# The conditioning vector's load moved to the ScalarE DMA queue, ahead of a transformer block on one core

## The chip, the cores and the metric

The kernel runs on one core of a Trainium2 chip. The metric is the device time of one execution, in microseconds (us). Each execution also has a span: the time from the first to the last recorded activity on the core, some 2.4 us shorter than the device time here. The span can be compared with times inside the trace.

## The reference

The block is a conditioned transformer block in bf16, with 2048 tokens and a width of 1024. A vector `c` is turned into six rows of modulation (shift, scale and gate for each of the two halves):

```python
mod = (silu(c) @ w_mod).reshape(1, 6, 1, -1)
sa, ca, ga, sb, cb, gb = mod[:, 0], ..., mod[:, 5]
h = layernorm(x) * (1 + ca) + sa
x = x + ga * linear_attention(h, wqkv, wo)      # 32 heads, phi(t) = elu(t) + 1
h = layernorm(x) * (1 + cb) + sb
x = x + gb * ((silu(h @ w_gate) * (h @ w_up)) @ w_down)   # width 3584
```

Only the opening matters here: the first row tiles of `x` (128 tokens each) are normalised, transposed, scaled with `ca`, shifted with `sa`, and multiplied by the Q part of `wqkv`.

## The kernel before

The kernel records its operations in a list, works out the semaphores, and emits one program per engine in the order of recording. All loads come from one queue, SyncE's, in this order:

```python
P.dma("c", CS8[0:NDT, :], cv8)                       # the vector, 2 KB
for st in range(4):
    P.dma("x0_%d" % st, XRES[:, st, :], xv[:, st, :])  # four x tiles, 256 KB each
ca_load(0)          # 1 MB of w_mod, columns of ca ("wca")
wq_load(0, 2)       # 512 KB of wqkv
ca_load(1)
wq_load(2, 2)
sa_load(1)          # 1 MB of w_mod, the upper half of sa ("wsa")
wq_load(4)          # 256 KB each
...                 # wq_load 5, 6, 7
sa_load(0)
# ... further x tiles and the K part of wqkv
```

The vector is transposed by TensorE, goes through Silu on ScalarE and is copied by VectorE. Then come the statistics of the x tiles, and between them TensorE runs "fillers": matmuls on zeros, whose result nobody reads, to keep it active.

```python
P.pe("transpose", out=PSB[:, 1, 0:NDT], in_=CS8[0:NDT, :], identity=IDENT[0:NDT, 0:NDT])
P.act("activation", out=SILUC[:], in_=PSB[:, 1, 0:NDT], func=ACT.Silu)
P.dve("tensor_copy", out=SILUF[:], in_=SILUC[:])
# ...
act_stats(2)                 # tile 2: sums on ScalarE
# ...
warm(13, bank=3)             # 13 fillers
# ... statistics of tiles 0 and 1 on VectorE, tile 0 normalised
tile_transposes(0)
warm(5, bank=3)              # 5 fillers
# ... tile 1 normalised on ScalarE
tile_transposes(1)
warm(1, bank=3)              # 1 filler
# ... tiles 2 and 3 normalised
mod_sc(WCA, 8, range(2))     # first modulation matmuls: silu(c) with ca's columns
fin_ca(0, 2)
tile_transposes(2, 3)
```

After this the Q matmuls follow, with more modulation matmuls between them. The first shift matmuls (`mod_sc` on `WSA`, columns 512 to 767) stand behind 26 of the Q matmuls and need the load `sa_load(1)`.

## Time and profile before

| | kernel before |
|---|---|
| device time, median of 3 | 836.26 us (834.89 to 836.29) |
| span of the profiled execution | 833.0 us |
| TensorE busy | 821.9 us, 99% |
| chain that ended last | 94% TensorE |
| TensorE idle before its first instruction | 2.2 us |

These are the head of the profile page, its busy times by engine, and its last chain, for the kernel before. "PEclk" on the page is at full rate in all slices. (The trace's first clock event, the grant of the full rate, is at 6.59 us; the page takes the time before it as full too.)

```profile
span 833.0 us, 10031 instructions
PE 821.9 (99%) x4053; PEld 379.9 (46%) x4132; DVE 301.7 (36%) x659; ACT 196.2 (24%) x335; POOL 43.6 (5%) x56
PE 94%; DVE 3%; DMA 1%; SPq 1%; issue 1%; ACT 0%; DVEq 0%; ACTq 0%
```

TensorE (PE) bounds the kernel. A change of the opening can only win what TensorE loses there. The timeline of the opening shows it. Its columns are: start in us, duration in us, engine, source line, operation, what it writes `<-` what it reads, shape and count; in brackets the idle time just before it on its engine, and what ended that. "SPq" is SyncE issuing a DMA.

```profile
0.79 0.40 SPq L178 DMA_DIRECT2D cs<-in_c_dram  x1
1.24 1.78 SPq L178 DMA_DIRECT2D xres<-in_A_x_dram  x4
2.42 0.18 ACT L178 ACTIVATE siluc<-ps 128x8 bf16<-128x8 bf16 x1 [0.35 <-PE ps L178]
4.03 1.94 DVE L178 BATCH_NORM_STATS2 stats<-xres 128x6 f32<-128x512 bf16 x3 [1.23 <-DMA xres<-in_A_x_dram]
6.28 1.06 ACT L178 ACTIVATE ht<-xres 128x1024 bf16<-128x1024 bf16 x1 [3.68 <-DMA xres<-in_A_x_dram]
8.79 0.56 SPq L178 DMA_DIRECT2D wsa<-in_w_mod_dram  x1
...
10.50 0.38 PE L178 MATMUL ps<-e,ident 128*128 128x512 bf16 x1
10.93 0.55 PE L178 MATMUL ps<-siluc,wca 128*128 128x1 bf16 x16
20.08 0.55 PE L178 MATMUL ps<-siluc,wsa 128*128 128x1 bf16 x16 [0.44 <-DMA wsa<-in_w_mod_dram]
28.42 1.89 PE L178 MATMUL ps<-ht,wqk 128*128 128x512 bf16 x8
```

Read from the top: the vector's issue holds SyncE for 0.40 us, and the x tiles' issues start at 1.24 us. VectorE waits for x until 4.03 us, and ScalarE waits for tile 2 until 6.28 us. TensorE waits 0.44 us for the shift weights at 20.08 us. From the last line on, TensorE runs without a wait of note to the end, which comes 833.0 - 28.42 = 804.6 us later. I call that line the end of the opening.

The windows view says what the loads do meanwhile. Its columns are: the window, its length, busy time of PE, PEld, DVE, ACT and POOL, the granted TensorE clock, the busy share of the DMA engines, and GB/s.

```profile
4.00:6.00 2.00, 2.00 (x6) 0.76 (x5) 1.97 (x4) 0.00 (x0) 0.00 (x0) 1.00 0.95 285
10.00:12.00 2.00, 1.89 (x34) 1.42 (x35) 1.24 (x4) 0.00 (x0) 0.78 (x1) 1.00 1.07 376
```

The DMA engines are full (share 0.95 and 1.07), and the loads land in the order of their issue: the first load of `wca` is complete at 10.88 us, the upper half of `wsa` at 20.04 us.

### The profile page before, as it was taken

Reading aid. Unit: us, or ns where it says so; the run is one execution under the profiler, and the core shown is the slowest. Engines: PE = TensorE matmul, PEld = TensorE weight load, DVE = VectorE, ACT = ScalarE, POOL = GpSimd, SP = SyncE. Lnnn points to the kernel's source line nnn. Section 1 sums busy time; section 2 is a strip of 40 time slices with the busy share of each in tenths; the row PEclk is TensorE's granted clock in tenths of the full one; section 3 lists DMA queues with packets and bytes.
Section 4 is the critical chain, followed back from the end, with each engine's and each line's share of the span. In section 5 each row is a group of like instructions: output and inputs, shape, how many; then the busy total and the mean of one; then the engine's idle time right before and its main releaser. Section 6 shows DMA issues by size and latency. Waiting matters only on the chain.

```text
span 833.0 us, 10031 instructions
## 1 busy us (share of the span) xinstructions
PE 821.9 (99%) x4053; PEld 379.9 (46%) x4132; DVE 301.7 (36%) x659; ACT 196.2 (24%) x335; POOL 43.6 (5%) x56
## 2 busy tenths in 40 slices
PE   7999999999999999999999999999999999999998
PEld 4544444454444444444444444444444444444444
DVE  5797985657873211110222211122111212111111
ACT  3667642223332111110211111111111111111011
POOL 1000000000050000030000003000000300000000
PEclk9999999999999999999999999999999999999999
DMA  9969734928197995610455571045557004553000
GB/s 312 298 149 228 205 74 146 200 103 303 34 222 241 255 272 152 177 51 13 114 152 152 151 186 42 13 113 153 152 152 198 28 13 119 152 154 93 1 26 25
DMA packets 190940, 117.17 MB, mean 141 GB/s; under 512 B 49576, under 2 KB 174640, under 8 KB 190896
## 3 DMA queue, kind: packets, MB, share of 16 engines
q1 hardware_dynamic: 190896, 116.55, 50.7%
q8 instruction: 32, 0.52, 0.3%
q14 instruction: 12, 0.10, 0.0%
HBM read 100.67 MB, written 4.33 MB: 126 GB/s over the span
## 4 chain that ended last, share of the span: by engine, by line
PE 94%; DVE 3%; DMA 1%; SPq 1%; issue 1%; ACT 0%; DVEq 0%; ACTq 0%
PE ps L178 94%; DMA wsa<-in_w_mod_dram 1%; DVE acc L178 1%; SPq L178 1%; DVE xres L178 0%; DVE pkt L178 0%; DVE mhl L178 0%; DVE ht L178 0%; DVE e L178 0%; DVE pqt L178 0%; ACT e L178 0%; ACT mw L178 0%; DVE ve L178 0%; DVE modcol L178 0%; DVE ut L178 0%
## 5 line engine op out<-in xcount | busy, mean ns | idle before, releaser
L178 PE MATMUL ps<-h2t,guu 128*128 128x512 bf16 x878 | 210.1, 379 | 0.9
L178 PE MATMUL ps<-h2t,gug 128*128 128x512 bf16 x878 | 209.9, 379 | 0.9
L178 DVE TENSOR_TENSOR at<-sg,ps 128x512 bf16<-128x512 bf16 x112 | 77.0, 687 | 296.2 <-PE ps L178 285.1
L178 ACT ACTIVATE sg<-ps 128x512 bf16<-128x512 f32 x112 | 66.9, 597 | 310.3 <-PE ps L178 298.9
L178 PEld LDWEIGHTS ps<-h2t,guu 128*128 128x128 bf16 x896 | 87.7, 98 | 105.7
L178 PEld LDWEIGHTS ps<-h2t,gug 128*128 128x128 bf16 x896 | 87.5, 98 | 105.3
L178 PE MATMUL ps<-wd_a,at 128*128 128x512 bf16 (+2 forms) x519 | 112.8, 372 | 0.5
L178 PE MATMUL ps<-ht,wqk 128*128 128x512 bf16 x498 | 110.7, 379 | 1.0 <-DVE ht L178 0.3
L178 PE MATMUL ps<-wd_b,at 128*128 128x512 bf16 (+2 forms) x388 | 85.4, 372 | 0.5
L178 PEld LDWEIGHTS ps<-wd_a,at 128*128 128x128 bf16 x528 | 51.1, 98 | 59.8
L178 PEld LDWEIGHTS ps<-ht,wqk 128*128 128x128 bf16 x512 | 49.3, 98 | 58.7 <-DVE mv L178 0.3
L178 DVE TENSOR_TENSOR ut<-att,gb_b 128x512 bf16<-128x512 bf16 (+1 forms) x32 | 13.8, 432 | 167.3 <-ACT att L178 167.3
L178 ACT ACTIVATE att<-ps 128x512 bf16<-128x512 f32 (+1 forms) x32 | 17.4, 591 | 182.1 <-PE ps L178 182.1
L178 PEld LDWEIGHTS ps<-wd_b,at 128*128 128x128 bf16 x396 | 38.3, 98 | 44.6
L178 PE MATMUL ps<-pk,xres 128*128 128x512 bf16 x250 | 56.2, 379 | 0.4 <-issue 0.2
L178 PE MATMUL ps<-mw,pqt 128*128 128x512 bf16 x250 | 55.8, 379 | 0.4
L178 POOL TENSOR_SCALAR h2t<-h2t,modcol 128x512 bf16<-128x512 bf16 x32 | 28.6, 912 | 394.9 <-DMA h2t<-xn 378.6
L178 ACT ACTIVATE e<-ps 128x512 bf16<-128x512 f32 x56 | 33.0, 602 | 32.8 <-PE ps L178 27.3
L178 PEld LDWEIGHTS ps<-mw,pqt 128*128 128x128 bf16 x256 | 24.9, 98 | 29.7 <-DVE xres L178 0.2
L178 PEld LDWEIGHTS ps<-pk,xres 128*128 128x128 bf16 x256 | 24.8, 98 | 29.8 <-issue 0.4
L178 ACT ACTIVATE junk<-xres 128x1024 bf16<-128x1024 bf16 x24 | 25.4, 1059 | 36.0 <-DVE xres L178 35.8
L178 POOL TENSOR_TENSOR rstd<-ve,neghalf 128x1 f32<-128x1 f32 (+2 forms) x17 | 14.2, 850 | 215.7 <-DVE ve L178 176.4
(101 smaller groups left out, 342.5 us busy)
## 6 DMA issues: line engine op xcount, KB each, us to landing
gug<-in_B_w_gate_dram SPq DMA_DIRECT2D x56, 512.0 KB, 4.0
guu<-in_B_w_up_dram SPq DMA_DIRECT2D x56, 512.0 KB, 5.3
xres<-in_A_x_dram SPq DMA_DIRECT2D x20, 256.0 KB, 8.0
rb<-recip_den SPq DMA_DIRECT2D x8, 512.0 KB, 11.9
stgx<-in_w_mod_dram SPq DMA_DIRECT2D x2, 2048.0 KB, 8.8
wd_a<-in_B_w_down_dram SPq DMA_DIRECT2D x4, 1024.0 KB, 7.5
out_dram<-xres SPq DMA_DIRECT2D x31, 128.0 KB, 1.7
xres<-in_A_x_dram SPq DMA_DIRECT2D x3, 1024.0 KB, 14.5
```

Source lines behind the costliest of these rows:

```text
L178: return getattr(e, method)(**kw)
```

## The change

Its intent: the vector's issue leaves SyncE's queue, so that the first x tile heads it; and a filler goes that would then stand in the way. The short description speaks of "the first filler matmuls", but the diff drops one filler, the third group; the 13 and the 5 stay. The rest of the diff is bookkeeping: since ScalarE now also issues a DMA, a recorded operation carries a flag for "is a DMA" where the engine's name used to tell.

```diff
-        P.dma("c", CS8[0:NDT, :], cv8)
+        P.dma("c", CS8[0:NDT, :], cv8, queue="act")
@@
-        warm(1, bank=3)
+        warm(0, bank=3)
@@ bookkeeping, one of several places
-            if op.eng not in self.COMPUTE and op.fn is not None:
+            if op.isdma and op.fn is not None:
```

In the built program the vector's load is ScalarE's first instruction, ahead of its table load and of Silu.

More of the change, by code (lines that the diff above doesn't have):

```diff
@@ L96 @@
 class _Op:
-    __slots__ = ("idx", "eng", "fn", "deps", "signaled", "count", "semkey", "waits", "ninc", "tag")
+    __slots__ = ("idx", "eng", "fn", "deps", "signaled", "count", "semkey", "waits", "ninc", "tag", "isdma")
     def __init__(self, idx, eng, fn, semkey, ninc, tag):
@@ L109, in __init__ @@
         self.tag = tag
+        self.isdma = semkey.startswith("lane:")
 def _is_ap(v):
@@ L129, in add @@
     def add(self, eng, fn, reads=(), writes=(), lane=None, ninc=1, tag=None):
-        if eng in self.COMPUTE:
-            semkey = eng
-        else:
-            assert lane is not None
-            semkey = "lane:" + lane
+        semkey = eng if lane is None else "lane:" + lane
+        assert eng in self.COMPUTE or lane is not None
         op = _Op(len(self.ops), eng, fn, semkey, ninc, tag)
@@ L165, in add @@
         self.by_eng.setdefault(eng, []).append(op)
-        if eng not in self.COMPUTE:
+        if op.isdma:
             self.dma_ops.append(op)
@@ L216, in resolve @@
             if op.signaled:
-                c = counters.get(op.semkey, 0) + (op.ninc if op.eng in self.COMPUTE else 16 * op.ninc)
+                c = counters.get(op.semkey, 0) + (16 * op.ninc if op.isdma else op.ninc)
                 counters[op.semkey] = c
@@ L236, in resolve @@
                 sn = dict(kn)
-                if op.eng in self.COMPUTE:
+                if not op.isdma:
                     sn[op.semkey] = op.count
@@ L253, in body @@
                     if op.signaled:
-                        if eng in self.COMPUTE:
+                        if not op.isdma:
                             r.then_inc(sems[op.semkey], op.ninc)
```

## The prediction

> **What bounds it.** The page gives a span of 833.0 us with TensorE busy 821.9 us (99%) at the full granted clock; the chain that ended last is 94% TensorE. From about 20 us to the end TensorE hardly waits: the waits view lists only some 4.5 us of TensorE idle time worth naming, 2.2 us of it before the first instruction, none over 0.2 us after 21 us. In the opening 20 us the loads bound it: the windows view shows the DMA share at 0.94 to 1.09 from 3 us on (240 to 380 GB/s), and the chain of waits over the first 45 us runs through SyncE's issues and the load of the shift weights (wsa) to 20.04 us.
>
> **What the change does.**
> 1. The conditioning vector's issue (0.79 us, 0.40 us long on SyncE) leaves the SyncE queue. The x tiles, issued from 1.24 us, and all loads after them then move up by 0.45 us. [...] I count only that; the trace of before has one issuing engine, so it cannot confirm it.
> 2. ScalarE gets the issue, ahead of its first table load (1.28 us, now at 0.79). Silu (now at 2.42) comes 0.2 to 0.4 us later. VectorE needs the Silu result for its copy (2.63 us) ahead of the first statistics; those wait for x until 4.03 us, about 3.6 us after the change. About 0.5 us of slack is left, so no cost.
> 3. Though the title says fillers, the diff drops only one, between the transposes of tile 1 and the first modulation matmuls (10.50 us, 0.38 us). The weight load behind it was released by wca at 10.93 us, so dropping it alone gains nothing; it only clears the way once wca lands near 10.5 us.
>
> **How it adds up.** x lands about 0.45 us earlier, so statistics, tile 2's sums on ScalarE (started by x at 6.28 us) and the transposes of tile 1 (10.05 us, released by ScalarE) move up alike. wca lands about 0.45 earlier, wsa too (TensorE waits for it at 20.08 us). The transposes of tile 0 gain only 0.2 us (the 13 fillers still end at 7.61 us), hidden behind the wait for ScalarE. Clock warm-up: fillers stand about 0.43 us apart until 6.6 us, then 0.27 or less. [...] it is untouched. From 20 us on everything keeps its length and is shifted.
>
> Gain about 0.45 us of 836 (0.05%), below the scatter of the three runs (834.89 to 836.29). The runs average about 835.8; I predict 835.4 us, range 834.2 to 836.6; faster by over 2% 0.005, within 2% 0.99, slower 0.005.
>
> **What would show each step.** The timeline: first x issue near 0.8 us; first statistics near 3.6 us instead of 4.03; first modulation matmul near 10.5 instead of 10.93; first shift matmul near 19.6 instead of 20.08. TensorE's busy time falls by about 0.4 us.
>
> **What would make it wrong.** The vector landing late on the ScalarE queue (behind x packets), which would hold the fillers and the VectorE copy and thus the statistics; the first x transfer not starting earlier because something other than the issue sets the first arrival; another packet interleaving that delays wca or wsa. Each is tenths of a us.

The sum is the 1.24 - 0.79 = 0.45 us by which the x issue moves up. The fillers' spacing changes at 6.6 us, and the trace of before has the grant of the full clock at 6.59 us.

## The result

The changed kernel took 834.90 us in the median (834.55 to 835.88, 4 runs), the kernel before 835.62 us in the median of its 4 runs of that comparison. The ratio is 0.9993 with a 95% interval of 0.9976 to 1.0011. Ratios here are the mean time of one kernel's fast runs over that of the other's of the same rounds, so they are not quite the ratio of the medians.

The profiled execution was the slowest of the four. Its page:

```profile
span 833.4 us, 10108 instructions
PE 825.8 (99%) x4131; PEld 379.8 (46%) x4131; DVE 301.9 (36%) x659; ACT 196.0 (24%) x335; POOL 43.3 (5%) x56
PE 96%; DMA 1%; DVE 1%; SPq 1%; issue 0%; ACT 0%; DVEq 0%
```

TensorE's busy time did not fall by 0.4 us, it rose by 3.9 us. That shows no cost: the count of recorded matmuls rose from 4053 to 4131 although one matmul was dropped. The trace of before lacks 79 records (4132 weight loads, 4053 matmuls). Busy sums of these two traces can't be compared to a few tenths.

The timeline of the opening, changed kernel, same execution ("ACTq" is ScalarE issuing a DMA):

```profile
0.79 1.82 SPq L176 DMA_DIRECT2D xres<-in_A_x_dram  x4
0.79 0.58 ACTq L176 DMA_DIRECT2D cs<-in_c_dram  x1
2.70 0.18 ACT L176 ACTIVATE siluc<-ps 128x8 bf16<-128x8 bf16 x1
3.66 1.88 DVE L176 BATCH_NORM_STATS2 stats<-xres 128x6 f32<-128x512 bf16 x3 [0.58 <-DMA xres<-in_A_x_dram]
6.31 1.06 ACT L176 ACTIVATE ht<-xres 128x1024 bf16<-128x1024 bf16 x1 [3.44 <-DMA xres<-in_A_x_dram]
7.95 0.59 SPq L176 DMA_DIRECT2D wsa<-in_w_mod_dram  x1
...
10.28 0.54 PE L176 MATMUL ps<-siluc,wca 128*128 128x1 bf16 x16
20.43 0.55 PE L176 MATMUL ps<-siluc,wsa 128*128 128x1 bf16 x16 [0.76 <-DMA wsa<-in_w_mod_dram]
28.77 1.45 PE L176 MATMUL ps<-ht,wqk 128*128 128x512 bf16 x6
```

The first steps are as predicted: x is issued at 0.79 us, the statistics start 0.37 us earlier, the first modulation matmul 0.65 us earlier. But tile 2 reaches ScalarE no earlier (6.31 against 6.28 us), and wsa, issued 0.84 us earlier, releases TensorE 0.35 us later. So this execution's opening ends 0.35 us later than in the trace of before. From there to the end it takes 833.4 - 28.77 = 804.6 us, as before. The windows view of the changed kernel shows the DMA engines full as well:

```profile
4.00:6.00 2.00, 2.00 (x6) 0.76 (x5) 1.97 (x6) 0.00 (x0) 0.01 (x1) 1.00 0.99 332
10.00:12.00 2.00, 1.29 (x32) 1.15 (x30) 1.18 (x4) 0.00 (x0) 0.78 (x1) 1.00 1.10 352
```

The questions were: is the head start real, what is it worth, and why is it not in this trace?

### The profile page after: what moved, and what is told of

Read it like the earlier page. It is cut to its first block, busy times and chain, and to the rows that moved or that the text cites. A ratio compares the mean times of both kernels' runs of the same rounds, so it can differ in the third digit from the quotient of the medians.

```text
span 833.4 us, 10108 instructions
## 1 busy us (share of the span) xinstructions
PE 825.8 (99%) x4131; PEld 379.8 (46%) x4131; DVE 301.9 (36%) x659; ACT 196.0 (24%) x335; POOL 43.3 (5%) x56
## 4 chain that ended last, share of the span: by engine, by line
PE 96%; DMA 1%; DVE 1%; SPq 1%; issue 0%; ACT 0%; DVEq 0%
PE ps L176 96%; DMA wsa<-in_w_mod_dram 1%; SPq L176 1%; DVE acc L176 0%; DVE xres L176 0%; DVE mhl L176 0%; ACT mw L176 0%; DVE ve L176 0%; DVE ut L176 0%; DVE mean L176 0%; DVE msq L176 0%; DVE sumx L176 0%; DVEq L247 0%
```

## The experiments

Theory "shift": everything moves by the time that the head of the queue was held. Rival "absorption": the opening waits for loads whose landing scatters more than the head start, so that the gain is lost. All kernels gave the right result. The record has the span of every execution of the experiments, and in all traces the rest after the opening takes 804.6 to 804.7 us, so the span tells to about 0.1 us when the opening ended.

### The same two kernels again

Edit: none. `after_again` and `after_third` are the changed kernel, `before_again` is the kernel before.

> The changed kernel again, unedited. Shift theory (all loads and all work move up by the 0.45 us that the vector's issue took): mean time 0.3 to 0.6 us below the kernel before, and in the trace the first shift matmul (wsa) starts between 19.4 and 19.8 us. Absorption theory (the opening waits for loads whose landing scatters by more than the head start; in the first trace of after wsa landed at 20.4 us although it was issued 0.84 us earlier): the mean is within 0.2 us of before, and the wsa matmul starts anywhere from 19.5 to 20.5 us.

> The kernel before again, unedited, as a measure of noise: ratio 1.000 within 0.0007 (0.6 us). Its trace shows how much the landing of x tile 2 (6.28 us in the first trace) and of wsa (20.04 us) scatter with nothing changed: absorption theory 0.3 us or more, shift theory below 0.15 us.

> The changed kernel a third time, for the size of the gain: the span lies 0.3 to 0.6 us below that of the kernel before in the mean (shift theory, 0.45), and every execution's span follows from where the opening ended, so that the time from the bias matmuls to the end is 804.5 to 804.8 us as in all traces so far.

| run | median us | before, same chip | ratio, 95% | spans |
|---|---|---|---|---|
| after_again | 834.81 | 835.34 | 0.9999 (0.9987 to 1.0012) | 831.8 to 835.0 |
| before_again | 834.96 | 835.34 | 0.9997 (0.9985 to 1.0008) | 832.4 to 833.2 |
| after_third | 835.35 | 835.27 | 1.0006 (0.9993 to 1.0018) | 832.4 to 834.8 |

One comparison can't resolve the effect. Taken together, over the executions whose spans the record lists (those of the experiments, and the first four of the changed kernel): two of 45 executions of the kernel before and two of 15 of the changed one have a mean granted clock of 0.998 instead of 1.000 and spans of 834.8 to 835.3 us. They are treated below (see the dose experiment); both kernels have them. Without them the mean span is 832.87 us for the kernel before (43 executions, standard error 0.06) and 832.57 us for the changed one (13, standard error 0.14): a gain of 0.30 us, with a 95% interval of about 0.0 to 0.6. With them the difference of the means is 0.09 us, and is not resolved. The figure also pools chips. On chip 4 the changed kernel's five full-clock executions are 0.58 us below the 16 of the kernel before; on chip 12 its four are 0.11 us above the nine. So the size of the gain rests on few executions.

In the traces, the end of the opening was 28.42 and 28.11 us for the kernel before, and 28.77, 27.64 and 28.96 us for the changed one. The earliest parts moved every time: the first statistics started at 4.03 and 4.02 us before, and at 3.66, 3.67 and 3.56 us after. The first shift matmul did not: 20.08 and 19.77 us before, 20.43, 19.30 and 20.61 us after. `before_again` showed scatter of 0.2 us in tile 2 (6.50 against 6.28 us) and 0.3 us in that matmul, with nothing changed. So the first step of "shift" holds and the last one depends on one load's landing, as "absorption" has it.

### Each half alone

`act_only` keeps the filler:

```diff
 # against the changed kernel
-        warm(0, bank=3)
+        warm(1, bank=3)
```

> Only the vector's move to the ScalarE queue; the single filler stays. Both theories: the same time as the changed kernel within 0.2 us, since the filler stands in a gap. Rival (the filler matters): 0.3 to 0.4 us slower than the changed kernel, because once wca lands near 10.2 us the filler of 0.38 us is in the way of the first modulation matmuls and nothing hides it.

`filler_only` leaves the vector on SyncE and drops the filler:

```diff
 # against the kernel before
-        warm(1, bank=3)
+        warm(0, bank=3)
```

> Only the filler is dropped; the vector stays on the SyncE queue. Prediction: no gain, within 0.2 us of the kernel before, because the modulation matmuls behind it wait for wca at 10.9 us anyway. Rival (the filler was on the path): 0.3 to 0.4 us faster than before.

Measured: `act_only` 834.61 us, ratio 0.9993 (0.9981 to 1.0005), mean span 832.24 us; `filler_only` 835.07 us, ratio 0.9999 (0.9987 to 1.0011), mean span 832.76 us. Against the 16 executions of the kernel before on the same chip, `act_only` gains 0.62 us and `filler_only` 0.10 us (standard errors about 0.2). So the gain sits with the vector's move, and the filler is worth nothing measurable, in either place; it stands in a gap. The timeline of `act_only` shows why: tile 1's transposes come after a wait, and behind them the filler ends 10.32 + 0.38 = 10.70 us, where the first modulation matmul (10.64 us, pipelined behind it) could not have started before 10.60 us, when the last part of wca landed. Where wca lands sooner, as in the first trace of the changed kernel, TensorE then idles in front of the next step: it waited 0.71 us for VectorE before the transposes of tiles 2 and 3.

```profile
9.86 0.62 PE L176 MATMUL ps<-ident,xres 128*128 128x128 bf16 x8 [0.83 <-ACT xres L176]
10.32 0.38 PE L176 MATMUL ps<-e,ident 128*128 128x512 bf16 x1
10.64 0.55 PE L176 MATMUL ps<-siluc,wca 128*128 128x1 bf16 x16
```

### The dose: more tiny loads at the head

If 0.45 us at the head are worth 0.45 us at the end, then extra issues there must cost as much. They are loads of the same 2 KB vector into unused places.

```diff
 # against the kernel before; head4 has range(4)
         P.dma("c", CS8[0:NDT, :], cv8)
+        for i in range(8):
+            P.dma("cx%d" % i, T("cx%d" % i, 192 * KB + 256 * i, [128, 128], BF16)[0:NDT, :], cv8)
```

> The kernel before with eight more tiny loads (the same 2 KB vector, into unused places) at the head of the SyncE queue: a dose eight times the cost that the change removes. Shift theory: the first x issue moves from 1.24 us to about 4.7 us, and the whole program ends later by 8 times 0.43, 3.4 us, give or take 0.5. Absorption theory (the opening waits for something other than the head of the queue): under 1.5 us later.

> Half the dose of the earlier run: four extra tiny loads at the head of the SyncE queue. That run showed 0.335 us for each and an end 0.95 us later per us of delay at the head; on that line four give 1.3 us later than the kernel before (1.0 to 1.6). If small delays are absorbed by the scatter of the loads, under 0.7 us.

| run | x first issued | median us | ratio, 95% | mean span over that of before, same chip |
|---|---|---|---|---|
| kernel before | 1.24 us | | | |
| head4 | 2.58 us (+1.34) | 836.65 | 1.0020 (1.0007 to 1.0032) | 834.24 - 832.77 = +1.47 us |
| head8 | 3.94 us (+2.70) | 837.50 | 1.0030 (1.0016 to 1.0043) | 835.52 - 832.99 = +2.54 us |

I had taken 0.43 us for each extra issue; a repeated tiny one takes 0.29 us and a gap of 0.05, so the dose was smaller than written down for `head8`. Per microsecond at the head the end came 1.1 and 0.94 us later. The second figure includes a lower clock in three of the four executions of `head8`, as the next paragraph shows; its one execution at full clock came 835.2 - 832.99 = 2.2 us later, 0.8 us per us. Delays of this size at the head go through about in full, which is what "shift" says, and "absorption" of them is out. The dose adds delay only: it does not show that the 0.45 us taken away comes back in full.

`head8` also shows what a clock of 0.998 is. In three of its four executions, the profiled one among them, the mean granted clock was below 1.000. Its windows view:

```profile
9.00:11.00 2.00, 0.67 (x9) 0.56 (x10) 1.92 (x6) 1.97 (x4) 1.31 (x2) 1.00 1.08 376
11.00:13.00 2.00, 1.98 (x11) 0.89 (x10) 1.83 (x7) 1.24 (x2) 0.99 (x2) 0.64 1.07 376
13.00:15.00 2.00, 2.00 (x31) 1.73 (x29) 0.86 (x3) 0.00 (x0) 0.34 (x1) 0.51 1.09 352
15.00:17.00 2.00, 2.00 (x32) 1.36 (x30) 1.34 (x4) 1.38 (x2) 0.00 (x0) 1.00 1.08 367
```

TensorE had idled 1.96 us ahead of 10.33 us, and its clock was then at half rate from 11.54 to 14.96 us, for 3.41 us (by the trace's clock events). That costs (1 - 0.64) x 2 + (1 - 0.51) x 2 = 1.7 us of clock, which is 0.002 of the span. The four outliers of the unedited kernels have the same mean clock of 0.998 and come out about 2.3 us longer; none of them was the profiled execution, so that they have the same cause is likely, not shown. In `head4`, with the same idle stretch of 1.96 us in its trace, all five executions kept the full clock, so what brings the half rate on is not shown.

### The vector behind the x tiles, on SyncE

Does it take the second queue? The x tiles would also head SyncE's queue if the vector were simply put behind them.

```diff
 # against the kernel before; also warm(1, bank=3) -> warm(0, bank=3)
-        P.dma("c", CS8[0:NDT, :], cv8)
         for st in range(4):
             P.dma("x0_%d" % st, XRES[:, st, :], xv[:, st, :])
+        P.dma("c", CS8[0:NDT, :], cv8)
```

> The changed kernel, but the vector stays on SyncE and is merely put behind the four x tiles. If the ScalarE queue were not needed, this would be as fast as the changed kernel (x heads the queue too). My theory: the vector lands behind 1 MB of x, at 5.5 to 7 us; the fillers and VectorE's copy ahead of the first statistics wait for it, and the end is 2 to 4.5 us later than in the changed kernel.

Measured: 837.60 us, ratio 1.0029 (1.0015 to 1.0043). The vector's first reader started at 5.83 us, and VectorE's first statistics at 6.34 us instead of 3.6 us:

```profile
5.83 0.18 PE L178 MATMUL ps<-ident,cs 8*128 8x8 bf16 x1 [5.83 <-DMA cs<-in_c_dram]
5.94 4.29 PE L178 MATMUL ps<-e,ident 128*128 128x512 bf16 x13
6.26 0.17 DVE L178 CAST siluf<-siluc 128x8 f32<-128x8 bf16 x1 [3.56 <-ACT siluc L178]
6.34 1.87 DVE L178 BATCH_NORM_STATS2 stats<-xres 128x6 f32<-128x512 bf16 x3
```

Its mean span is 835.22 us, 2.65 us over the changed kernel's full-clock mean and 2.24 us over the kernel before on the same chip. The tiny load needs to be early, because program order puts everything behind it; the second queue lets it be early without holding the first (in the changed kernel its issue and the x issue both start at 0.79 us).

### A second x tile on the second queue

```diff
 # against the changed kernel
-            P.dma("x0_%d" % st, XRES[:, st, :], xv[:, st, :])
+            P.dma("x0_%d" % st, XRES[:, st, :], xv[:, st, :], queue="act" if st == 2 else "sp")
```

> The changed kernel with x tile 2, which starts ScalarE's chain (at 5.8 to 6.3 us), issued on the ScalarE queue behind the vector, at about 1.4 us as before but with tile 3 and all weights one issue (0.47 us) earlier on SyncE. If issue time at the head is what counts, another 0.2 to 0.4 us gain; if from 3 us on the transfers themselves fill the engines (share 0.95 to 1.1), no gain beyond 0.2 us.

Measured: 834.75 us, ratio 0.9995 (0.9983 to 1.0008), mean span 832.44 us: no gain over the changed kernel that could be told from noise. Tile 2 landed at 6.23 us, no earlier than in the changed kernel (5.77 to 6.29 us in its three traces), and tile 1, which came in shortly before it, landed at 6.05 us instead of 4.16 to 4.49 us, so that VectorE waited for it:

```profile
6.08 0.69 DVE L176 BATCH_NORM_STATS2 stats<-xres 128x6 f32<-128x512 bf16 x1 [1.22 <-DMA xres<-in_A_x_dram]
```

So a whole tile on the second queue brought nothing here that could be told from noise, although wca and the loads after it were issued earlier (wca's first issue at 2.17 us here, 2.65 us in `after`).

### The load that TensorE waits for, in two parts

```diff
 # against the changed kernel, in sa_load(p)
-            P.dma("wsa%d" % p, WSA[:, :, 512 * p:512 * p + 512], wmv[:, :, 512 * p:512 * p + 512])
+            for h in range(2 if p == 1 else 1):
+                c0, n_ = (512 * p + 256 * h, 256) if p == 1 else (0, 512)
+                P.dma("wsa%d%d" % (p, h), WSA[:, :, c0:c0 + n_], wmv[:, :, c0:c0 + n_])
```

> The changed kernel with the load that TensorE waited for in the first trace (wsa, columns 512 to 1023) cut into two loads of 256 columns, of which the first matmuls need the first alone. If the landing of wsa sets the end of the opening in the slow executions: first shift matmul never later than 19.5 us, mean 0.2 to 0.5 us below the changed kernel, and less scatter (0.3 us instead of 0.6). If x tile 2's chain sets it: same mean within 0.2 us.

Measured: 835.36 us, ratio 0.9999 (0.9986 to 1.0013), spans 832.2 to 833.0 us. The first shift matmul came at 18.82 us without a wait, but the wait moved down the queue, to the lower half of the shift weights:

```profile
18.82 0.54 PE L176 MATMUL ps<-siluc,wsa 128*128 128x1 bf16 x16
25.63 0.95 PE L176 MATMUL ps<-siluc,wsa 128*128 128x1 bf16 x32 [0.30 <-DMA wsa<-in_w_mod_dram]
```

The scatter was somewhat less (standard deviation of the span 0.32 us in five executions, against 0.51 us in the changed kernel's 13), the mean no better: a miss. Speeding one load left the next one to wait for. One run can't say that the split did it: in this trace the part that fell back across the fetch (next section; 1.4 to 1.8 us in every trace) was one of the second of the two loads, not of the first.

### Why wsa lands late: what the completion events show

The traces record 16 completions for each of these loads; I call them its parts. TensorE went on when the last had come: wsa's last part came at 20.04 us in `before` and at 20.38 us in `after`, and the first shift matmul, which needs it, started at 20.08 and 20.43 us. The table has the median (the ninth of the 16) and the last part, in us, for wsa and for the load issued just before it ("wq23", 512 KB, row blocks 2 and 3 of the Q weights), both taken from the traces' completion events. "Lag" is last minus median. "Fetch" is the start of a single packet of 16 KB, of the kind "instruction", which runs for 1.05 to 1.19 us in every trace.

| trace | wq23 median, last, lag | wsa median, last, lag | lag grew by | fetch |
|---|---|---|---|---|
| before | 14.96, 16.64, 1.68 | 17.94, 20.04, 2.10 | 0.42 | 16.84 |
| before_again | 15.03, 15.89, 0.86 | 18.01, 19.72, 1.71 | 0.85 | 17.20 |
| filler_only | 14.95, 16.64, 1.69 | 17.94, 20.50, 2.56 | 0.87 | 17.17 |
| after | 14.51, 15.84, 1.33 | 17.51, 20.38, 2.87 | 1.54 | 17.21 |
| after_again | 14.64, 16.19, 1.55 | 17.62, 19.26, 1.64 | 0.09 | 16.71 |
| after_third | 14.71, 16.08, 1.37 | 17.67, 20.57, 2.90 | 1.53 | 16.70 |
| act_only | 15.06, 16.34, 1.28 | 18.15, 19.27, 1.12 | -0.16 | 16.63 |
| x2_act | 15.48, 15.78, 0.30 | 18.47, 20.34, 1.87 | 1.57 | 17.74 |
| no_fill (below) | 14.65, 15.94, 1.29 | 17.67, 18.95, 1.28 | -0.01 | 19.57 |
| fill32 (below) | 14.97, 15.69, 0.72 | 17.98, 18.69, 0.71 | -0.01 | 18.86 |

Two things are in it. The bulk of wsa did move: the median part landed at 17.94 and 18.01 us in the kernel before and at 17.51, 17.62 and 17.67 us in the changed one. `act_only`, with its median at 18.15 us, seems to contradict, but the mean of all 16 parts is steadier: 18.17, 18.19 and 18.22 us where the vector heads SyncE (`before`, `before_again`, `filler_only`), 17.65, 17.73 and 17.91 us in the changed kernel, 18.05 us in `act_only`. So the head start reached the bulk of this load, with about 0.4 us. But the last part, which TensorE waits for, did not follow.

What happened shows when each load's 16 completion times are sorted and compared with those of the load before it. From the first load of `wca` to the lower half of the shift weights (ten loads), the pattern of the 16 stays the same from load to load, within 0.16 us, with one exception in each trace: across the fetch, exactly one part falls 1.4 to 1.8 us behind the others (best match of the two patterns). This holds in all 14 traces, the four that are not in the table included. It is in wsa where the fetch runs while wsa moves, and in a later load where the fetch comes later (`no_fill`, `fill32`, `late_c_sp`).

What differs is which part is hit. In `after`, `after_third` and `x2_act` it was the part that came last anyway, and the lag grew by all of it. In `act_only` it was one of the first six, and nothing was lost. In the two traces of before it was about the 13th and the tenth, which then became the last. The openings fit: they ended at 28.72 to 28.96 us in `after`, `after_third`, `x2_act` and `filler_only` (one of its last four parts was hit), and at 27.64 and 27.65 us in `after_again` (about the eighth) and `act_only`. The traces do not say which DMA engine served a part, so what ties the late part to the fetch is the coincidence, 14 times in 14, and the two experiments below that move the fetch.

The third trace of the changed kernel has the longest wait:

```profile
20.61 0.55 PE L176 MATMUL ps<-siluc,wsa 128*128 128x1 bf16 x16 [1.31 <-DMA wsa<-in_w_mod_dram]
```

The DMA view of the changed kernel, for 16 to 19 us, has it as queue 8; in the same window `no_fill` has no such line:

```profile
q1 hardware_dynamic: 752, 1.10, 105.0%
q8 instruction: 1, 0.02, 2.4%
```

(Packets, MB, share of 16 engines' time: 2.4% of 16 engines for 3 us is 1.15 us of one engine.) The trace gives the packet's kind and size, not what it carries. That it is a fetch of TensorE's program is my estimate, by the count. The page of every run has the same line for the whole execution:

```profile
q8 instruction: 32, 0.52, 0.3%
```

32 packets of 16 KB stand against some 8200 recorded matmuls and weight loads, and from the first to the last they are on average some 250 of these apart; no other engine has more than 831 records. The first one starts when TensorE has put out some 120 to 130 matmuls (recorded: 120 to 132), be that at 16.8 us or, in `head8`, at 19.7 us. (The expectation of `fill32` below says that all traces but one had it at 16.6 to 17.9 us; `head8` and `late_c_sp`, 18.88 us, did not either.)

### All fillers dropped

```diff
 # against the changed kernel
-        warm(13, bank=3)
+        warm(0, bank=3)
-        warm(5, bank=3)
+        warm(0, bank=3)
```

> The changed kernel with all fillers dropped (13 and 5 as well), which the title of the change could be read to say. If the fillers before the first transposes are what brings TensorE to full rate in time: the first Q matmuls still stand 0.43 us apart, and the end is 1 to 3 us later, with more scatter. If they do nothing: same time within 0.3 us.

Measured: 835.75 us, ratio 1.0008 (0.9994 to 1.0021), mean span 833.26 us, 0.7 us over the changed kernel's full-clock mean: in the direction expected, but less than the 1 us that was named. Against the same chip it is 0.5 us over the kernel before (standard error 0.2), and 0.4 us over the changed kernel's four full-clock executions, which is not resolved. The transposes of a tile take 1.04 us instead of 0.62 us, those of tiles 2 and 3 together 2.17 us instead of 1.25 us, and the first Q matmuls are slow too; then they run at full rate. The clock events agree: the full rate was granted at 13.59 us here, and at 5.45 to 8.68 us in all traces with fillers. So the 18 fillers bring the full clock forward, which is probably what the lost time is; the nineteenth filler is worth nothing measurable. This trace has the other observation too: with 18 matmuls and their weight loads fewer in TensorE's program the fetch came 2.4 to 2.9 us later than in the changed kernel, behind wsa.

```profile
7.32 1.04 PE L176 MATMUL ps<-ident,xres 128*128 128x128 bf16 x8 [4.58 <-DVE xres L176]
10.78 2.17 PE L176 MATMUL ps<-ident,xres 128*128 128x128 bf16 x16
19.98 0.54 PE L176 MATMUL ps<-siluc,wsa 128*128 128x1 bf16 x16
```

### Fewer, longer fillers: move the fetch, keep the clock

```diff
 # against the changed kernel
-        P.dve("memset", ap=E1[:, 0, :], constant=0.0)
+        FZ = T("fz", 184 * KB, [128, 512], FP32)
+        P.dve("memset", ap=FZ[:], constant=0.0)
-                P.pe("matmul", out=PS[:, bank, :], lhsT=IDENT[:], rhs=E1[:, 0, :], start=True, stop=True)
+                P.pe("matmul", out=PS[:, bank, :], lhsT=FZ[:, 0:128], rhs=FZ[:], start=True, stop=True)
-        warm(13, bank=3)
+        warm(3, bank=3)
-        warm(5, bank=3)
+        warm(1, bank=3)
```

> The changed kernel with the 18 fillers (13 and 5, bf16) replaced by 4 (3 and 1) in float32, on the guess that each keeps TensorE busy several times as long, so that 14 matmuls and their weight loads leave TensorE's program before the shift weights are needed. In all traces but one a 16 KB transfer of kind instruction runs for 1.1 us at 16.6 to 17.9 us, just while wsa moves; in the trace without fillers it came at 19.6 us, after wsa, and wsa's last part landed at 18.95 us instead of 19.3 to 20.6. Fetch theory (this transfer sometimes holds up the engine that ends last): it comes at 19 us or later here, wsa is complete by 19.3 us, and no execution has the long wait; if the clock is released as before, the span is 832.0 to 832.6 us with little scatter. Rival (wsa's late landing is the loads' own scatter): span as the changed kernel, 832.7 in the mean, and wsa anywhere up to 20.6 us.

Measured: 834.74 us, against 835.33 us for the kernel before; ratio 0.9987 (0.9974 to 1.0001); spans 831.9 to 833.0 us, mean 832.37. The float32 fillers were recorded as two matmuls each (6 in 5.49 us, so the first three took 1.83 us each, against 0.43 us from one bf16 filler to the next in the kernel before until 6.57 us), so only 10 matmuls left the program; the fetch came at 18.86 us, not quite the 19 us that I had named, but behind the last part of wsa (18.69 us). TensorE did not wait for wsa's upper half, and in the profiled execution the load then moving got the lag: wq5 went to 2.10 us of lag from 0.70 us for wq4, and TensorE waited for the lower half of the shift weights.

```profile
18.86 0.54 PE L176 MATMUL ps<-siluc,wsa 128*128 128x1 bf16 x16
25.79 0.95 PE L176 MATMUL ps<-siluc,wsa 128*128 128x1 bf16 x32 [0.89 <-DMA wsa<-in_w_mod_dram]
```

So the fetch can be moved, and the late part moves with it, here as in `no_fill`; with the one late part at the fetch in every trace, that shows the fetch theory as far as traces without the name of the DMA engine can. It does not make a faster kernel for certain: the mean is 0.2 us below the changed kernel's full-clock mean, within the noise, and the ratio's interval just reaches 1 (two of the kernel before's executions in that comparison were 0.998-clock outliers, which flatter it). No version here is shown to beat the changed kernel.

## Why the prediction was right, and where it was off

The prediction (835.4 us, 834.2 to 836.6) holds: 834.90 us in the first comparison. The time alone tests little, since the kernel before (835.62 us there) lies in the stated range too; and that these two medians differ by more than predicted, 0.72 us, is luck: two of the four executions of before were at 836.3 us. What can be tested are the steps.

1. *TensorE bounds the kernel and only the opening has slack.* Right. In every trace the stretch from the end of the opening to the end is 804.6 to 804.7 us.
2. *The x issue moves from 1.24 to about 0.8 us, at no cost on ScalarE.* Right: 0.79 us. The vector's issue took ScalarE 0.57 to 0.59 us, where it had taken SyncE 0.39 to 0.40 us. Silu moved from 2.42 to 2.70 us (0.2 to 0.4 predicted), the vector's copy was done by 3.07 us, and VectorE still waited 0.58 us for x after it.
3. *Only issue time is counted as saved.* Right as far as tested: the dose experiment gives 0.8 to 1.1 us at the end per us at the head, and putting a whole tile on the second queue gave nothing more (mean span 832.44 us, against 832.57 us).
4. *The filler alone gains nothing.* Right (`filler_only`, `act_only`).
5. *Statistics at about 3.6 us, first modulation matmul at about 10.5 us.* Right: 3.56 to 3.67 us and 10.28 to 10.51 us (10.93 and 10.69 us in the two traces of before).
6. *"wca lands about 0.45 earlier, wsa too", first shift matmul near 19.6 us.* Off. The first shift matmul stood at 20.43, 19.30 and 20.61 us. The bulk of wsa came about 0.4 us earlier, its last part did not: it landed at 19.26 to 20.57 us (19.72 and 20.04 us before). The step that failed is to treat a load's landing as a fixed delay from its issue. It is the last of 16 parts, and in every trace one part falls back by 1.4 to 1.8 us across a fetch that is not in the kernel's text. The 20.08 us from which the prediction counted was itself set by such a hit. The prediction's own list of what would make it wrong has "another packet interleaving that delays wca or wsa", but sizes it at tenths of a us.
7. *The gain of 0.45 us.* Right within what can be measured, probably somewhat large: 0.30 us (0.0 to 0.6) for the changed kernel over full-clock executions; pooled with `act_only`, which differs only by the filler, 832.87 - 832.48 = 0.39 us (standard error 0.13). What is missing, if anything, may have gone to point 6 in the executions where wsa's last part was late; that is not shown.
8. *TensorE's busy time falls by 0.4 us.* Not testable: the records missing from the trace of before are worth more.

What stays open: what decides which of the 16 parts the fetch hits, why that part falls back by 1.4 to 1.8 us when the packet runs for 1.05 to 1.19 us, and whether the rare 0.998-clock executions of the two unedited kernels have any link to the change (2 of 45 executions against 2 of 15 is too few to tell).

## What to carry to other kernels

Here the DMA engines were full from 3 us on (share 0.94 to 1.09 in the kernel before), and a delay of the first issue went through to the end almost one to one: 1.34 us came out as 1.47 us, 2.70 us as 2.54 us (2.2 us in its one execution at full clock). The tiny load that other work needs early was best on a second issuing queue: ahead of the bulk it cost about 0.3 us (0.0 to 0.6), behind it 2.65 us; beyond that issue time the second queue brought nothing that could be told from noise. In a similar opening that is the place to try first. A load ended when the last of its 16 parts ended, and in every trace here one part fell back by 1.4 to 1.8 us across a fetch (of TensorE's program, by my estimate): before an effect of tenths of a microsecond is read from one trace, look at how the part that is waited for scatters in two traces of the same kernel, and use the spans of all executions.
